# Retiming the later batches of a fused retention and Fourier-mixing kernel, with more of the ReLU on ScalarE

## The chip, the cores and the metric

One core of one Trainium2 chip. The metric is the device time of one execution in microseconds (us). A kernel's time is the median of its executions. Engines are named as the profile names them: PE (TensorE), PEld (its weight loads), DVE (VectorE), ACT (ScalarE), POOL (GpSimd) and SP, whose queue (SPq) issues almost all transfers. A "psh product" is a matmul of the first layer, a "psc product" one of the second; "wkA" is the score product q k^T.

## The reference, cut to what matters

```python
# retention: q, k, v are (4 batches, 8 heads, 768 steps, 64), float32
for t in range(S):
    state = gamma * state + outer(k[:, :, t], v[:, :, t])
    y[:, :, t] = scale * q[:, :, t] @ state
x = y.transpose(0, 2, 1, 3).reshape(B, S, 512)
# Fourier mixing, normalisation and a two-layer MLP with residual
u  = x + real(fft(fft(x, axis=1), axis=2))
un = (u - mean(u)) / sqrt(var(u) + 1e-6)
out = u + relu(un @ w_ch1) @ w_ch2        # w_ch1 512x2048, w_ch2 2048x512
```

The kernel computes the recurrence in chunks: scores of 128 x 128 under a decay mask, and a running state. The Fourier transform is a set of products with cosine and sine tables. Tiles are float16, sums float32. The attention of batch b+1 is woven into the MLP of batch b. That is why nearly all products are ready in time, and why the order of instructions decides where PE waits.

## The kernel before

Units of work are put into one order by time slots: every stream of units gets a start and an end in "batches", and the units are sorted by slot. Each engine then works through its own instructions in that order, as far as the scheduler of the build leaves it. The parts that the change touches:

```python
    def load_unit(b, i, after=None):
        def run():
            h0 = 2 * PAIR_ORDER[i]
            for name, src in srcs.items():
                t = inp.tile([P, 2, NCH, D], f32, tag="in32", name=f"{name}32")
                rows = "h (p c) d -> p h c d" if b < NPE and name == "q" else \
                    "h (c p) d -> p h c d"
                dma = nc.sync.dma_start(t, src[b, h0:h0 + 2].rearrange(rows, p=P))
                if after is not None:
                    tc.add_manual_dep(dma.ins, w_dma[after].ins.name,
                                      mybir.DependencyInfo(mybir.DependencyClass.Sync,
                                                           mybir.DependencyReason.DATA),
                                      reason="loads in turn")
                in_of[name, b, i] = t
        return run
    # ... cut ...
    def t_unit(b, i):
        def run():
            st = at[b, i] = {}
            kT = st["kT"] = tp.tile([P, NCH, P], f16, tag="kT", name="kT")
            if b >= NPE:
                qT = st["qT"] = qts[i % 2]
                nc.sync.dma_start_transpose(qT.rearrange("p h c t -> p (h c) t"),
                                            q16_of[b, i].rearrange("p h c d -> p (h c d)"))
                nc.sync.dma_start_transpose(kT, kd_of[b, i].rearrange("p c h d -> p (c h d)"))
                return
    # ... cut ...
    def a_unit(b, i, part):
        def run():
            st = at[b, i]
            if part == 0:
                st["atm"] = ap_.tile([P, NCH, 2, P], f16, tag="atm", name="atm")
            wk = ps_g.tile([P, 2, 2, P], f32, tag="g", name="wkA")
            for c2 in range(2):
                c = 2 * part + c2
                nc.tensor.matmul(wk[:, c2], st["kT"][:, c, :], st["qT"][:, :, c, :],
                                 start=True, stop=True)
            nc.vector.tensor_tensor(
                out=st["atm"][:, 2 * part:2 * part + 2], in0=wk,
                in1=maskp[:, PAIR_ORDER[i]].unsqueeze(1).to_broadcast([P, 2, 2, P]),
                op=ALU.mult)
        return run
    # ... cut ...
            if b == 0 and kb < 3:
                for c0, c1 in (((0, 256), (256, DM)) if kb == 0 else ((0, DM),)):
                    una = nc.scalar.activation(un[:, c0:c1], u[:, kb, c0:c1], AF.Identity,
                                               bias=fd[0]["mu"][:, kb:kb + 1], scale=-1.0)
                lb[b]["bst", kb] = bst
    # ... cut ...
    def unT_unit(b, kb):
        def run():
            un, unT = lb[b].pop(("un", kb)), lb[b]["unT"]
            if b >= NPE:
                nc.sync.dma_start_transpose(unT[:, :, kb * P:(kb + 1) * P], un)
                return
            pst = ps_g.tile([P, 4, P], f16, tag="g", name="pst", padded_shape=[P, 8, P])
            for cb in range(4):
                nc.tensor.transpose(pst[:, cb, :], un[:, cb * P:(cb + 1) * P], ident16)
            if b == 0 and kb == 0:
                nc.scalar.copy(unT[:, 0:2, 0:P], pst[:, 0:2])
                nc.scalar.copy(unT[:, 2:4, 0:P], pst[:, 2:4])
            elif (kb % 2 == 0) != (b == 0 and kb < 3):
                nc.vector.tensor_copy(unT[:, :, kb * P:(kb + 1) * P], pst)
            else:
                nc.scalar.copy(unT[:, :, kb * P:(kb + 1) * P], pst)
        return run
    # ... cut ...
    def h_unit(b, rt, fb):
        def run():
            unT = lb[b]["unT"]
            psh = ps_pm.tile([P, 384], f32, tag="pm", name="psh", padded_shape=[P, DM])
            for cb in range(4):
                nc.tensor.matmul(psh, w116[:, cb, fb * P:(fb + 1) * P],
                                 unT[:, cb, rt * 384:(rt + 1) * 384],
                                 start=(cb == 0), stop=(cb == 3))
            if fb % 2 == 0:
                nc.scalar.activation(ht16[:, fb, :], psh, AF.Relu, bias=0.0, scale=-1.0)
            else:
                nc.vector.tensor_scalar(out=ht16[:, fb, :], in0=psh, scalar1=-1.0, scalar2=0.0,
                                        op0=ALU.mult, op1=ALU.max)
        return run
    # ... cut ...
    def ch_unit(b, rt, rb3, part):
        def run():
            rb = rt * 3 + rb3
            if part == 0:
                psc_of[0] = ps_pm.tile([P, DM], f32, tag="pm", name="psc")
            psc = psc_of[0]
            for fb in range(4 * part, 4 * part + 4):
                nc.tensor.matmul(psc, ht16[:, fb, rb3 * P:(rb3 + 1) * P], w216[:, fb, :],
                                 start=(fb == 0), stop=(fb == NFB - 1))
            if part == 3:
                ob = obp.tile([P, DM], f32, tag="ob", name="ob")
                nc.vector.scalar_tensor_tensor(out=ob, in0=psc, scalar=lb[b]["st"][:, rb, 3:4],
                                               in1=lb[b]["u"][:, rb, :], op0=ALU.mult,
                                               op1=ALU.add)
                nc.sync.dma_start(out[b, rb * P:(rb + 1) * P, :], ob)
        return run
    # ... cut ...
    def emit(streams):
        ev = []
        for si, (units, t0, t1) in enumerate(streams):
            for i, u in enumerate(units):
                ev.append((t0 + (t1 - t0) * (i + 1.0) / len(units), si, i, u))
        ev.sort(key=lambda e: e[:3])
        for e in ev:
            e[3]()
            if e[0] < 1.0:
                behind()
                pin(None if e[0] < 0.05 else ["Pool", "GpSimd"])
    # ... cut ...
        t0 = b + (0.1 if b == 0 else 0.0)
        s2s, unTs = mix_units(b, [3, 4, 5])
        streams += [(majors, b, b + 1.0), (s2s, t0 + 0.02, t0 + 0.14),
                    (unTs, t0 + 0.2, t0 + 0.28)]
        if b + 1 < B:
            steps = attn_steps(b + 1)
            if b == 0:
                streams.append(([load_unit(1, i, 6) for i in range(4)], -0.1, 0.0))
                streams.append(([qt_zeros], 0.1, 0.15))
                streams.append(([pad_unit], 0.9, 0.95))
                ts = (0.28, 0.33, 0.38, 0.46, 0.55, 0.63, 0.69, 0.75)
            else:
                streams.append(([load_unit(b + 1, i) for i in range(4)], b - 0.3, b + 0.15))
                n = [len(u) for u in steps]
                ts = [0.04 + 0.55 * sum(n[:j]) / sum(n) for j in range(7)]
                ts.insert(1, ts[1])
            streams.append((steps[0], b + ts[0], b + ts[1]))
            streams += [(u, b + ts[j + 2], b + ts[j + 3]) for j, u in enumerate(steps[1:])]
            end = b + ts[-1]
            streams.append(([s1_unit(b + 1, 0, 1), s1_unit(b + 1, 1, 1)], end + 0.02, end + 0.04))
            s2s, unTs = mix_units(b + 1, [0, 1, 2])
            t1, t2 = (0.13, 0.19) if b == 0 else (0.17, 0.23)
            streams += [(s2s, end + 0.06, end + t1), (unTs, end + t1 + 0.01, end + t2)]
    emit(streams)
```

`load_unit` loads q, k and v of a pair of heads; in batch 2 (b = 1) the loads wait only for the seventh weight load. `t_unit` transposes q (after ACT's cast to float16) and k, for batches 3 and 4 by DMA on SP's queue. `h_unit` is one block of the first layer, whose ReLU goes in turn to ACT and DVE. `ch_unit` is one row block of the second layer, with one eviction of 512 columns and one write at its end. `csn_unit` (not shown) makes one of three small cosine tables on ACT. A `filler` is one product without use that keeps PE working.

## Time and profile before

| | kernel before |
|---|---|
| median of 4 runs beside the changed kernel | 262.43 us (261.95 to 264.47) |
| span in the profiled run | 260.5 us, clock 1.00 |
| first product of the first layer starts at | 34.99 us |
| last product of the second layer ends, roughly | 256.6 us |
| waits for transposed q at wkA | 1.61 + 0.93 + 0.46 = 3.0 us idle |

To read it: PE is nearly always busy, so only the places where it waits can be won. The prediction lists them by stage. The idle time in brackets in a timeline is the time before an instruction in which its engine did nothing, and behind the arrow stands what ended it. One reading is used all through this document, and the prediction derives it: **a stage's loss** is the sum of start-to-start distances of its matmuls, less the time in which those matmuls stream without a pause (216 ns for 512 columns).

### The profile page before, as it was taken

Reading aid. Unit: us, or ns where it says so; the run is one execution under the profiler, and the core shown is the slowest. Engines: PE = TensorE matmul, PEld = TensorE weight load, DVE = VectorE, ACT = ScalarE, POOL = GpSimd, SP = SyncE. Lnnn points to the kernel's source line nnn. Section 1 sums busy time; section 2 is a strip of 40 time slices with the busy share of each in tenths; the row PEclk is TensorE's granted clock in tenths of the full one; section 3 lists DMA queues with packets and bytes.
Section 4 is the critical chain, followed back from the end, with each engine's and each line's share of the span. In section 5 each row is a group of like instructions: output and inputs, shape, how many; then the busy total and the mean of one; then the engine's idle time right before and its main releaser. Section 6 shows DMA issues by size and latency. Waiting matters only on the chain.

```text
span 260.5 us, 5236 instructions
## 1 busy us (share of the span) xinstructions
PE 241.7 (93%) x2020; PEld 145.7 (56%) x2020; DVE 182.5 (70%) x446; ACT 117.9 (45%) x244; POOL 73.1 (28%) x129
## 2 busy tenths in 40 slices
PE   6997899999998989799999998899999999999993
PEld 2454679656766536465566545655566455545541
DVE  7789867978998765897787726897787537423421
ACT  7898576653652345653144406551145315403300
POOL 6758302575100071570001604540003203100000
PEclk9999999999999999999999999999999999999999
DMA  8998999999999209999990185685110431311012
GB/s 172 264 248 136 204 202 207 234 245 261 267 216 224 60 0 248 165 201 185 260 238 3 40 191 117 117 113 131 43 40 0 60 121 25 43 72 49 0 43 81
DMA packets 97432, 35.99 MB, mean 138 GB/s; under 512 B 88192, under 2 KB 94336, under 8 KB 97408
## 3 DMA queue, kind: packets, MB, share of 16 engines
q1 hardware_dynamic: 93184, 31.47, 58.1%
q0 software_dynamic: 4224, 4.19, 9.9%
q8 instruction: 16, 0.26, 0.4%
q14 instruction: 8, 0.07, 0.1%
HBM read 27.26 MB, written 6.29 MB: 129 GB/s over the span
## 4 chain that ended last, share of the span: by engine, by line
PE 54%; DVE 18%; ACT 7%; POOL 7%; DMA 6%; SPq 3%; issue 3%; POOLq 0%; ACTq 0%
PE psc L896 23%; PE psh L859 16%; DMA qTz<-q16z 4%; SPq L153 3%; ACT x L627 3%; PE ps L685 3%; POOL u L795 3%; DVE atm L568 3%; DVE bst L812 2%; DMA k<-in_k_dram 2%; POOL u L793 2%; DVE xab L644 2%; PE wkA L566 2%; DVE ht L865 2%; DVE eo L654 2%
## 5 line engine op out<-in xcount | busy, mean ns | idle before, releaser
L896 PE MATMUL psc<-w,ht 128*128 128x512 f16 x384 | 89.7, 379 | 0.0
L859 PE MATMUL psh<-unT,w 128*128 128x384 f16 x448 | 82.7, 326 | 1.8 <-ACT ht L863 1.1
L859 PEld LDWEIGHTS <-w 128*128 128x128 f16 x448 | 42.6, 98 | 25.7 <-issue 2.8
L896 PEld LDWEIGHTS <-ht 128*128 128x128 f16 x384 | 36.5, 98 | 36.6
L863 ACT ACTIVATE ht<-psh 128x384 f16<-128x384 f32 x56 | 27.4, 488 | 53.9 <-PE psh L859 53.9
L793 POOL TENSOR_TENSOR u<-u,x 128x256 f32<-128x256 f32 x21 | 13.3, 635 | 125.7 <-DVE u L786 122.1
L865 DVE TENSOR_SCALAR ht<-psh 128x384 f16<-128x384 f32 x56 | 30.8, 551 | 11.7 <-PE psh L859 11.4
L900 DVE SCALAR_TENSOR_TENSOR ob<-psc,stats,u 128x512 f32<-128x512 f32 x24 | 17.9, 747 | 25.8 <-PE psc L896 25.8
L568 DVE TENSOR_TENSOR atm<-wkA,maskp 128x512 f16<-128x512 f32 x36 | 23.6, 681 | 2.1 <-PE wkA L566 2.1
L627 ACT ACTIVATE x<-wkY,gexp 128x384 f16<-128x384 f32 x24 | 12.8, 580 | 22.8 <-PE wkY L619 22.8
L814 ACT ACTIVATE un<-u,stats 128x512 f16<-128x512 f32 x21 | 15.1, 720 | 15.8 <-DVE stats L813 13.0
L812 DVE BATCH_NORM_STATS2 bst<-u 128x6 f32<-128x512 f32 x21 | 14.6, 695 | 9.4 <-POOL u L795 9.3
L594 DVE SCALAR_TENSOR_TENSOR s<-s,gkrow,wkK 128x128 f16<-128x128 f16 x48 | 16.3, 339 | 1.0
L566 PE MATMUL wkA<-qTz,kT 128*128 128x256 f16 x72 | 12.6, 272 | 3.2 <-DMA qTz<-q16z 3.0
L139 PE MATMUL wps<-ht 128*128 128x512 f16 x40 | 13.5, 444 | 2.2 <-POOL ht L184 2.2
L349 POOL TENSOR_SCALAR kd<-k,gexp 128x384 f16<-128x384 f32 x24 | 13.7, 583 | 1.8 <-DMA k<-in_k_dram 1.8
L795 POOL TENSOR_TENSOR u<-u,x 128x256 f32<-128x256 f32 x21 | 13.3, 635 | 2.5 <-DVE u L788 2.5
L786 DVE SCALAR_TENSOR_TENSOR u<-pq,g,qn 128x257 f32<-128x257 f32 x24 | 11.4, 475 | 3.4 <-ACT qn L783 3.4
L783 ACT COPY qn<-pq 128x255 f32<-128x255 f32 x24 | 8.8, 369 | 6.5 <-PE pq L774 5.7
L566 PEld LDWEIGHTS <-kT 128*128 128x128 f16 x72 | 6.8, 97 | 8.7 <-issue 4.7
L876 PE MATMUL psh<-unT,w 128*128 128x128 f16 x192 | 11.5, 219 | 0.1
L690 ACT CAST g<-ps 128x386 f16<-128x386 f32 x8 | 4.8, 600 | 14.9 <-PE ps L685 14.9
(144 smaller groups left out, 321.3 us busy)
## 6 DMA issues: line engine op xcount, KB each, us to landing
q<-in_q_dram SPq DMA_DIRECT2D x16, 384.0 KB, 6.1
k<-in_k_dram SPq DMA_DIRECT2D x16, 384.0 KB, 5.6
v<-in_v_dram SPq DMA_DIRECT2D x16, 384.0 KB, 6.3
out_dram<-ob SPq DMA_DIRECT2D x24, 256.0 KB, 2.3
w<-in_moe_w_ch_dram POOLq DMA_DIRECT2D x8, 512.0 KB, 10.9
unT<-un SPq DMA_TRANSPOSE x12, 2.5
kT<-kd SPq DMA_TRANSPOSE x8, 3.0
qTz<-q16z SPq DMA_TRANSPOSE x8, 4.1
```

The lines of the kernel that those rows point to most:

```text
L566: nc.tensor.matmul(wk[:, c2], st["kT"][:, c, :], st["qT"][:, :, c, :], start=True, stop=True)
L568: nc.vector.tensor_tensor(out=st["atm"][:, 2 * part:2 * part + 2], in0=wk, in1=maskp[:, PAIR_ORDER[i]].unsqueeze(1).to_broadcast([P, 2, 2, ...
L594: nc.vector.scalar_tensor_tensor(out=s16[:, c], in0=s16[:, c - 1], scalar=gkrow[:, hp, 1:2], in1=wk[:, c - c0], op0=ALU.mult, op1=ALU.add)
L627: nc.scalar.activation(dst, yk[h2], AF.Copy, bias=0.0, scale=gq8[:, h:h + 1])
L793: nc.gpsimd.tensor_tensor(out=u[:, kb, 0:256], in0=u[:, kb, 0:256], in1=x[:, kb, 0, 1:257], op=ALU.add)
L795: nc.gpsimd.tensor_tensor(out=u[:, kb, 256:512], in0=u[:, kb, 256:512], in1=x[:, kb, 1, 257:1:-1], op=ALU.add)
L812: nc.vector.bn_stats(bst, u[:, kb, :])
L859: nc.tensor.matmul(psh, w116[:, cb, fb * P:(fb + 1) * P], unT[:, cb, rt * 384:(rt + 1) * 384], start=(cb == 0), stop=(cb == 3))
L863: nc.scalar.activation(ht16[:, fb, :], psh, AF.Relu, bias=0.0, scale=-1.0)
L865: nc.vector.tensor_scalar(out=ht16[:, fb, :], in0=psh, scalar1=-1.0, scalar2=0.0, op0=ALU.mult, op1=ALU.max)
L896: nc.tensor.matmul(psc, ht16[:, fb, rb3 * P:(rb3 + 1) * P], w216[:, fb, :], start=(fb == 0), stop=(fb == NFB - 1))
L900: nc.vector.scalar_tensor_tensor(out=ob, in0=psc, scalar=lb[b]["st"][:, rb, 3:4], in1=lb[b]["u"][:, rb, :], op0=ALU.mult, op1=ALU.add)
```

## The change

The intent is to remove PE's waits in batches 2 to 4 without changing the arithmetic: (1) slots are shifted, above all so that the casts and DMA transposes of q come earlier (`ts`, loads, `da`, `dm`); (2) ACT takes 11 and 10 of each 16 ReLU blocks in place of 8, to relieve DVE; (3) the loads of batch 2 also wait for a product of the first batch, so that they do not compete with the weights; (4) the very last row block is done in two column halves, so that half of its eviction and write is out of the way early. At the start (5) the cosine tables move back to the end of the fourth pair, fillers are added, and the first centred row is no longer halved.

```diff
+ACT_ROWS = ((2, 3, 4, 5, 6, 7, 8, 9, 10, 13, 14), (0, 1, 4, 6, 7, 9, 10, 11, 12, 14))
@@ loads
-                    tc.add_manual_dep(dma.ins, w_dma[after].ins.name,
-                                      mybir.DependencyInfo(mybir.DependencyClass.Sync,
-                                                           mybir.DependencyReason.DATA),
-                                      reason="loads in turn")
+                    for x in (w_dma[after].ins, lb[0]["mm"].ins):
+                        tc.add_manual_dep(dma.ins, x.name,
+                                          mybir.DependencyInfo(mybir.DependencyClass.Sync,
+                                                               mybir.DependencyReason.DATA),
+                                          reason="loads in turn")
@@ first centred row of batch 1
-                for c0, c1 in (((0, 256), (256, DM)) if kb == 0 else ((0, DM),)):
-                    una = nc.scalar.activation(un[:, c0:c1], u[:, kb, c0:c1], AF.Identity,
-                                               bias=fd[0]["mu"][:, kb:kb + 1], scale=-1.0)
+                una = nc.scalar.activation(un, u[:, kb, :], AF.Identity,
+                                           bias=fd[0]["mu"][:, kb:kb + 1], scale=-1.0)
@@ its transposed copy
-            if b == 0 and kb == 0:
-                nc.scalar.copy(unT[:, 0:2, 0:P], pst[:, 0:2])
-                nc.scalar.copy(unT[:, 2:4, 0:P], pst[:, 2:4])
-            elif (kb % 2 == 0) != (b == 0 and kb < 3):
+            if (kb % 2 == 0) != (b == 0 and kb < 3):
@@ ReLU
-            if fb % 2 == 0:
+            if fb in ACT_ROWS[rt]:
@@ first layer of batch 1: remembers a product that the loads wait for
+            if (kb, g) == (1, 3):
+                lb[0]["mm"] = mm
@@ second layer: last row block in column halves
+            split = b == B - 1 and rb == NCH - 1
+            n = 2 if split else 4
+            if part % n == 0:
                 psc_of[0] = ps_pm.tile([P, DM], f32, tag="pm", name="psc")
             psc = psc_of[0]
-            for fb in range(4 * part, 4 * part + 4):
-                nc.tensor.matmul(psc, ht16[:, fb, rb3 * P:(rb3 + 1) * P], w216[:, fb, :],
-                                 start=(fb == 0), stop=(fb == NFB - 1))
-            if part == 3:
+            c0, c1 = (256 * (part // 2), 256 * (part // 2) + 256) if split else (0, DM)
+            k0 = NFB // n * (part % n)
+            for fb in range(k0, k0 + NFB // n):
+                nc.tensor.matmul(psc[:, c0:c1], ht16[:, fb, rb3 * P:(rb3 + 1) * P],
+                                 w216[:, fb, c0:c1], start=(fb == 0), stop=(fb == NFB - 1))
+            if part % n == n - 1:
                 ob = obp.tile([P, DM], f32, tag="ob", name="ob")
-                nc.vector.scalar_tensor_tensor(out=ob, in0=psc, scalar=lb[b]["st"][:, rb, 3:4],
-                                               in1=lb[b]["u"][:, rb, :], op0=ALU.mult,
+                nc.vector.scalar_tensor_tensor(out=ob[:, c0:c1], in0=psc[:, c0:c1],
+                                               scalar=lb[b]["st"][:, rb, 3:4],
+                                               in1=lb[b]["u"][:, rb, c0:c1], op0=ALU.mult,
                                                op1=ALU.add)
-                nc.sync.dma_start(out[b, rb * P:(rb + 1) * P, :], ob)
+                nc.sync.dma_start(out[b, rb * P:(rb + 1) * P, c0:c1], ob[:, c0:c1])
@@ start: the three csn units go from pairs 2 and 3 to the end of pair 4 (other moves cut)
-        un += a(1) + [csn_unit(0), filler(1), kv0_unit(1)] + e(1, *std) + [sc_unit(1)]
-        un += [q0_unit(2), t0_unit(2, 0), te_unit(2, 0), csn_unit(1), filler(3), k0_unit(2),
-               t0_unit(2, 1), te_unit(2, 1)]
+        un += a(1) + [filler(1), kv0_unit(1)] + e(1, *std) + [sc_unit(1)]
+        un += [q0_unit(2), t0_unit(2, 0), te_unit(2, 0), filler(3), k0_unit(2), t0_unit(2, 1),
+               te_unit(2, 1)]
# ... cut ...
+        un += a(3) + e(3, (0, 0), (1, 0)) + [kv0_unit(3), filler(4), sc_unit(3), t_act(4, 2),
+                                             csn_unit(0), csn_unit(1), csn_unit(2)]
# ... cut: four more fillers, folds in another order ...
@@ time slots of the streams
-        t0 = b + (0.1 if b == 0 else 0.0)
         s2s, unTs = mix_units(b, [3, 4, 5])
-        streams += [(majors, b, b + 1.0), (s2s, t0 + 0.02, t0 + 0.14),
-                    (unTs, t0 + 0.2, t0 + 0.28)]
+        dm = (0.12, 0.24, 0.3, 0.38) if b == 0 else (0.004, 0.140, 0.200, 0.341)
+        streams += [(majors, b, b + 1.0), (s2s, b + dm[0], b + dm[1]),
+                    (unTs, b + dm[2], b + dm[3])]
         if b + 1 < B:
             steps = attn_steps(b + 1)
             if b == 0:
-                streams.append(([load_unit(1, i, 6) for i in range(4)], -0.1, 0.0))
+                streams.append(([load_unit(1, i, 6) for i in range(4)], 0.180, 0.220))
                 streams.append(([qt_zeros], 0.1, 0.15))
-                streams.append(([pad_unit], 0.9, 0.95))
-                ts = (0.28, 0.33, 0.38, 0.46, 0.55, 0.63, 0.69, 0.75)
+                streams.append(([pad_unit], 0.900, 0.950))
+                ts = (0.249, 0.368, 0.424, 0.429, 0.545, 0.630, 0.695, 0.750)
             else:
-                streams.append(([load_unit(b + 1, i) for i in range(4)], b - 0.3, b + 0.15))
-                n = [len(u) for u in steps]
-                ts = [0.04 + 0.55 * sum(n[:j]) / sum(n) for j in range(7)]
-                ts.insert(1, ts[1])
+                streams.append(([load_unit(b + 1, i) for i in range(4)], b + -0.249, b + 0.044))
+                n = [len(u) for u in steps[1:]]
+                ts = [0.040, 0.044] + [0.044 + 0.550 * sum(n[:j]) / sum(n)
+                                         for j in range(6)]
             streams.append((steps[0], b + ts[0], b + ts[1]))
             streams += [(u, b + ts[j + 2], b + ts[j + 3]) for j, u in enumerate(steps[1:])]
             end = b + ts[-1]
-            streams.append(([s1_unit(b + 1, 0, 1), s1_unit(b + 1, 1, 1)], end + 0.02, end + 0.04))
+            da = (0.040, 0.048, 0.105, 0.135, 0.187, 0.237) if b == 0 else \
+                (0.068, 0.072, 0.054, 0.164, 0.174, 0.196)
+            streams.append(([s1_unit(b + 1, 0, 1), s1_unit(b + 1, 1, 1)], end + da[0],
+                            end + da[1]))
             s2s, unTs = mix_units(b + 1, [0, 1, 2])
-            t1, t2 = (0.13, 0.19) if b == 0 else (0.17, 0.23)
-            streams += [(s2s, end + 0.06, end + t1), (unTs, end + t1 + 0.01, end + t2)]
+            streams += [(s2s, end + da[2], end + da[3]), (unTs, end + da[4], end + da[5])]
```

More of the change, by code (lines that the diff above doesn't have):

```diff
@@ L875, in run @@
                 for cb in range(4):
-                    nc.tensor.matmul(psh[:, f], w116[:, cb, fb * P:(fb + 1) * P],
-                                     unT[:, cb, kb * P:(kb + 1) * P],
-                                     start=(cb == 0), stop=(cb == 3))
+                    mm = nc.tensor.matmul(psh[:, f], w116[:, cb, fb * P:(fb + 1) * P],
+                                          unT[:, cb, kb * P:(kb + 1) * P],
+                                          start=(cb == 0), stop=(cb == 3))
+            if (kb, g) == (1, 3):
+                lb[0]["mm"] = mm
             dst = ht16[:, 4 * g:4 * g + 4, kb * P:(kb + 1) * P]
@@ L891, in run @@
             rb = rt * 3 + rb3
-            if part == 0:
+            split = b == B - 1 and rb == NCH - 1
+            n = 2 if split else 4
+            if part % n == 0:
                 psc_of[0] = ps_pm.tile([P, DM], f32, tag="pm", name="psc")
             psc = psc_of[0]
-            for fb in range(4 * part, 4 * part + 4):
-                nc.tensor.matmul(psc, ht16[:, fb, rb3 * P:(rb3 + 1) * P], w216[:, fb, :],
-                                 start=(fb == 0), stop=(fb == NFB - 1))
-            if part == 3:
+            c0, c1 = (256 * (part // 2), 256 * (part // 2) + 256) if split else (0, DM)
[4 more added lines that the diff above has]
+            if part % n == n - 1:
                 ob = obp.tile([P, DM], f32, tag="ob", name="ob")
-                nc.vector.scalar_tensor_tensor(out=ob, in0=psc, scalar=lb[b]["st"][:, rb, 3:4],
-                                               in1=lb[b]["u"][:, rb, :], op0=ALU.mult,
+                nc.vector.scalar_tensor_tensor(out=ob[:, c0:c1], in0=psc[:, c0:c1],
+                                               scalar=lb[b]["st"][:, rb, 3:4],
+                                               in1=lb[b]["u"][:, rb, c0:c1], op0=ALU.mult,
                                                op1=ALU.add)
-                nc.sync.dma_start(out[b, rb * P:(rb + 1) * P, :], ob)
+                nc.sync.dma_start(out[b, rb * P:(rb + 1) * P, c0:c1], ob[:, c0:c1])
         return run
@@ L975, in first_units @@
                                                                      half_ids]
-        un += a(1) + [csn_unit(0), filler(1), kv0_unit(1)] + e(1, *std) + [sc_unit(1)]
-        un += [q0_unit(2), t0_unit(2, 0), te_unit(2, 0), csn_unit(1), filler(3), k0_unit(2),
-               t0_unit(2, 1), te_unit(2, 1)]
+        un += a(1) + [filler(1), kv0_unit(1)] + e(1, *std) + [sc_unit(1)]
+        un += [q0_unit(2), t0_unit(2, 0), te_unit(2, 0), filler(3), k0_unit(2), t0_unit(2, 1),
+               te_unit(2, 1)]
         un += y(1) + [td_dve(0), td_dve(1), yx_unit(1), filler(2)] + x(1) + [
             gk_unit(o[2]), t_act(3, 0), t_act(3, 1), v0_unit(2)]
-        un += a(2) + [filler(1), kv0_unit(2)] + e(2, *std) + [sc_unit(2), t_act(3, 2),
-                                                              csn_unit(2)]
+        un += a(2) + [filler(1), kv0_unit(2)] + e(2, *std) + [sc_unit(2), t_act(3, 2)]
         un += [q0_unit(3), w1_unit(0), t0_unit(3, 0), te_unit(3, 0), filler(3)] + y(2)
@@ L987, in first_units @@
         un += [w1_unit(g) for g in range(1, 4)] + [w2_unit(g) for g in range(4)]
-        un += a(3) + e(3, (0, 0), (1, 0)) + [kv0_unit(3), filler(4), sc_unit(3), t_act(4, 2)]
+        un += a(3) + e(3, (0, 0), (1, 0)) + [kv0_unit(3), filler(4), sc_unit(3), t_act(4, 2),
+                                             csn_unit(0), csn_unit(1), csn_unit(2)]
         un += e(3, (0, 1), (1, 1))
-        un += [yx_unit(3), yi_unit(3, 0), x0_unit(3, 0), filler(1), yi_unit(3, 1), x0_unit(3, 1),
+        un += [yx_unit(3), yi_unit(3, 0), x0_unit(3, 0), filler(2), yi_unit(3, 1), x0_unit(3, 1),
                g0_unit(0, (1,)), filler(1)]
-        un += [fold_s(0, 0, 130, 1, 2), fold_d(0, 0), s1_unit(0, 0, 0), fold_s(0, 130, 258, 1, 2),
-               px_unit(0), fold_d(0, 1, (0,)), xmean_unit(0), fold_d(0, 1, (1,)),
-               s1_unit(0, 1, 0), s1_unit(0, 0, 1), s1_unit(0, 1, 1), g0_unit(0, (2,)),
-               mean_unit(0)]
-        un += [s2_unit(0, 0), px_unit(1), s2_unit(0, 1), norm_unit(0, 0), gr_unit(0), gr_unit(1),
-               px_unit(2), filler(2), unT_unit(0, 0), xmean_unit(1), mean_unit(1),
+        un += [fold_s(0, 0, 130, 1, 2), fold_d(0, 0, (0,)), s1_unit(0, 0, 0),
+               fold_s(0, 130, 258, 1, 2), fold_d(0, 0, (1,)), fold_d(0, 1, (0,)), px_unit(0),
+               xmean_unit(0), fold_d(0, 1, (1,)), s1_unit(0, 1, 0), s1_unit(0, 0, 1),
+               s1_unit(0, 1, 1), px_unit(1), filler(1), g0_unit(0, (2,)), mean_unit(0)]
+        un += [s2_unit(0, 0), s2_unit(0, 1), norm_unit(0, 0), gr_unit(0), gr_unit(1),
+               px_unit(2), filler(4), unT_unit(0, 0), xmean_unit(1), mean_unit(1),
                norm_unit(0, 1), s2_unit(0, 2), xmean_unit(2), mean_unit(2), norm_unit(0, 2),
```

## The prediction

> **What bounds the kernel now.** I read the busy shares first, then the chain that ended last, then the busy times by stage, then TensorE's waits and its timeline around them.
>
> ```profile
> PE 241.7 (93%) x2020; PEld 145.7 (56%) x2020; DVE 182.5 (70%) x446; ACT 117.9 (45%) x244; POOL 73.1 (28%) x129
> ...
> PE 54%; DVE 18%; ACT 7%; POOL 7%; DMA 6%; SPq 3%; issue 3%; POOLq 0%; ACTq 0%
> ```
>
> TensorE is busy for 93% of the span and is the largest part of the last chain, but 46% of the chain lies elsewhere: the chain leaves TensorE wherever TensorE waits. A schedule change can win only those waits. The matmuls hardly change, so I must find the waits and see which of them the new order removes.
>
> ```profile
> 34.99:48.35 13.36, 13.11 (x212) 12.28 (x212) 9.24 (x23) 10.00 (x28) 2.72 (x8) 1.00 1.19 218
> 48.35:63.90 15.55, 14.46 (x121) 8.39 (x119) 12.69 (x31) 7.14 (x11) 10.36 (x15) 1.00 1.18 241
> 63.90:83.00 19.10, 18.22 (x206) 13.16 (x203) 17.74 (x46) 10.21 (x19) 1.98 (x3) 1.00 1.14 241
> 83.00:98.73 15.73, 14.43 (x94) 7.17 (x91) 11.49 (x27) 5.61 (x11) 5.61 (x9) 1.00 0.27 59
> 98.73:116.00 17.27, 15.33 (x129) 10.18 (x128) 13.71 (x34) 10.95 (x24) 9.42 (x15) 1.00 1.08 213
> ...
> 156.00:176.00 20.00, 18.53 (x159) 11.64 (x157) 16.37 (x41) 11.80 (x27) 9.42 (x15) 1.00 0.66 113
> 176.00:200.00 24.00, 23.14 (x193) 14.31 (x193) 18.49 (x43) 7.29 (x15) 1.23 (x2) 1.00 0.22 58
> ```
>
> Columns: stretch, its length, busy us of PE, PEld, DVE, ACT, POOL, clock, DMA share, GB/s. The clock is 1.00 throughout, so none of the loss is throttling. DVE is at 93% in 63.9-83 (17.74 of 19.10) and at 82% in 156-176, ACT at 53% and 59% there.
>
> Busy time hides part of each wait: a 512-column matmul is recorded as 379 ns, but 48 in a row take 10.36 us, 216 ns each, so about 0.16 us of drain covers the start of each pause. I therefore take each matmul's start-to-start distance in the timeline and subtract its streaming time (216 ns for 512 columns, 162 for 384, in proportion otherwise). What is left over per stage: 10.1 us before 35, then 0.9, 1.4, 1.7, 2.3, 2.65 (to 116), 1.1 (to 143), 0, 3.05 (156-176), 1.0, 1.0, and 0 from 225 on. From 35 to 256.6 that is 15.1 us; after the last matmul come 3.9 us of eviction and output.
>
> ```profile
> 107.60 0.38 PE L566 MATMUL wkA<-qTz,kT 128*128 128x256 f16 x2 [1.61 <-DMA qTz<-q16z]
> ...
> 163.11 0.38 PE L566 MATMUL wkA<-qTz,kT 128*128 128x256 f16 x2 [0.93 <-DMA qTz<-q16z]
> ...
> 176.61 0.38 PE L566 MATMUL wkA<-qTz,kT 128*128 128x256 f16 x2 [0.46 <-DMA qTz<-q16z]
> ```
>
> These three waits for a transposed q are the largest late ones: by start-to-start 1.77, 1.09 and 0.63 us, 3.5 in all. The chain shows the first:
>
> ```profile
> 101.28 0.92 PE psh L859 x6
> 102.20 5.26 DMA qTz<-q16z
> 107.47 0.14 issue
> ```
>
> The transpose needs 5.26 us from issue and is issued at 102.20 because ACT's cast of q16z ends only then, behind two ReLUs.
>
> **What the Trainium skill says.** (1) "TensorE: Matmul & The Clock Gate", Part 2, step 1: matmuls stay in program order, only weight loads are pulled ahead. So one waiting score product holds all ready first-layer products behind it; the trace agrees (1.61 us idle, then psh goes on). (2) The same page, Back-to-back issue gap, gives N/2.4 + 2.5 ns warm, 216 at N=512; the trace has 216. Halving 16 matmuls to 32 thus costs an estimated 16 x 2.5 = 40 ns. (3) "VectorE: DVE Perf Modes", The TRN2 errata, has (120+N)/0.96 ns for a PSUM source on VectorE and (172+N)/1.2 on ScalarE, 525 and 463 ns at 384 columns; the trace has 551 and 488, 5% more. (4) "Perfetto Trace Analysis", DMA Instruction HWDGE: the issuing record excludes data movement. The trace agrees: a q transpose is 1.5 us on the queue and 4.1 us to landing, so the landing counts.
>
> ```profile
> L863 ACT ACTIVATE ht<-psh 128x384 f16<-128x384 f32 x56 | 27.4, 488 | 53.9 <-PE psh L859 53.9
> ...
> L865 DVE TENSOR_SCALAR ht<-psh 128x384 f16<-128x384 f32 x56 | 30.8, 551 | 11.7 <-PE psh L859 11.4
> L900 DVE SCALAR_TENSOR_TENSOR ob<-psc,stats,u 128x512 f32<-128x512 f32 x24 | 17.9, 747 | 25.8 <-PE psc L896 25.8
> ```
>
> **The change part by part.** Positions below come from the built instruction order of both kernels, counted in matmul streaming time.
>
> q transposes ahead, batches 3 and 4. For batch 3 the first q cast moves on ACT ahead of the square root and the two ReLUs, so it ends some 3 us earlier, near 99, and the transpose lands near 104; the score product still comes 6.9 us of streaming after the stage's first product (7.0 before), near 105.7. The 1.77 us go. With the untangled groups (wkY no longer splits a psh group, after which 0.42 us waited for ACT) I book **2.0 of 2.65**. For batch 4 the cast and the transpose move into the previous batch; the third pair's product now comes 6.55 us after the buffer's last reader (5.5 before) against the 5.38 us which its DMA took plus hand-over. I book **2.3 of 3.05**.
>
> Second batch. Its first casts hold TensorE at 51.2-53 for 0.64 + 0.79 = 1.42 us; the transposes of q now come 4.8 us of streaming after the second layer starts, 2.8 before. **1.3**. The new load wait: loads started at 42.9, as soon as the seventh weight load landed, competing with the eighth until 44.5; the product named ends near 45. Of the 2 us delay about 1 is real for the stream, and the later casts have 3 to 5 us of slack before their transposes. **0**.
>
> ReLU mostly on ACT: 11 + 10 of 32 in place of 8 + 8. Over batches 2 to 4 that is 5 each and 2 in batch 1: 17 x 0.551 = 9.4 us off DVE, 17 x 0.488 = 8.3 us on ACT. Almost none of it is on the path by itself; it matters where DVE is full. In 63.9-83 one wait for a buffer costs 0.74 us and two for DVE 0.4 and 0.3: **0.9** of 1.7. In 116-143 and 176-200, four waits of 0.31 for atm or the folds: **0.6 + 0.6**. In 200-225: **0.4**. In 83-98.7 three waits for centred rows cost 1.58 us; their distance from the preceding products grows only by 0.3-0.6: **0.5**.
>
> Sum 2.0 + 2.3 + 1.3 + 0.9 + 1.2 + 0.4 + 0.5 = 8.6 us. Some waits will come back a few instructions later, since the chains behind them (u, POOL, bn_stats, ACT) are serial. I keep 85%: **7.3**.
>
> Column halves: the last eviction has 256 columns, 747 - 256/0.96 = 480 ns (estimate), 0.27 less; the last write has 128 KB, an estimated 0.25 less. Less 0.04: **0.5**.
>
> Costs. The three cosine-table activations (0.60 each, about 1.5 back to back) move from places where ACT had slack to right before the fourth pair's x, where ACT was idle 0.65 us: about **0.8** on the path to the first layer. Four more fillers are 4 x 0.216 = 0.86 us, mostly in idle time: **0.3**. ACT: in the first 15 us of batch 2's first half it now has 11 ReLUs (5.0 us at 0.45 back to back), 8 casts (3.7), 3 rows (2.0), 3 qn (1.1), x and unT (1.6): 13.4 of about 15.5 us, in order, with centred rows waiting on DVE among the ReLUs: **0.9** of new waits. Costs 2.0.
>
> Net 7.3 + 0.5 - 2.0 = 5.8 us: 262.4 - 5.8 = **256.6 us**.
>
> **Rivals.** *ACT takes DVE's place.* Runs of up to nine ReLUs in a row stand on ACT between centred rows that wait for statistics; if a row is late, three psh buffers are soon full and TensorE stops. For it: 13.4 of 15.5 us. Against: DVE, on which the rows wait, loses 1.65 us in the same stretch. It would give back 3 us or so: about 260. *Later transposes only move the wait.* The transposes share DMA with loads (213 GB/s in 98.7-116); if the earlier transpose takes 7 us rather than 5.3, half of the 3.5 us stays: about 258.5. *The full gain.* All stage losses but the 10 us at the start shrink to small change and cosines cost nothing: 15.1 less some 5, plus the tail: about 252.5.
>
> **Range and chances.** The first two rivals together would give about 261, the third 252.5; 8 in 10 I put at 253.3 to 260.3. Faster by 2% is below 257.1, just above my value: 0.54. Slower by 2% needs more new waits than all of ACT's added work: 0.02. The rest 0.44.
>
> **What would show it.** Right: no wait of wkA for qTz over 0.5 us; stage from first psh to the second layer of batch 2 near 15.3 us streaming plus 0.7; DVE near 173 us, ACT near 126; no wait over 0.3 us at tq of batch 2; first layer starts 0.5-1 us later than 34.99; last matmul to end 3.4 us. Wrong: psh waiting for ht on ACT by over 2 us in total (the first rival); transposes landing after 6 us and wkA still waiting (the second); first layer starting at 35 or before, with late losses under 6 us (the third).

## The result, and the profile after

The changed kernel takes **254.17 us** (median of 4 runs, 254.16 to 254.27) against 262.43 us beside it. It is correct. The ratio is 0.967, with a 95% interval of 0.962 to 0.972; a second measurement in five rounds gave 0.970 (0.969 to 0.971). Ratios here are the mean time of one kernel's fast runs over that of the other's fast runs of the same rounds, so not quite the ratio of the medians that are quoted. The gain is 8 us; 5.8 were predicted.

Busy shares, then the chain that ended last by engine, of the kernel after:

```profile
PE 237.9 (94%) x2040; PEld 147.7 (59%) x2040; DVE 176.1 (70%) x430; ACT 124.9 (49%) x259; POOL 73.1 (29%) x129
...
PE 68%; DVE 11%; ACT 7%; DMA 6%; POOL 3%; SPq 2%; issue 2%; ACTq 0%; DVEq 0%
```

PE's part of the last chain rose from 54% to 68% and DVE's fell from 18% to 11%: the chain leaves PE less often. PE's busy time fell by 3.8 us although it ran 20 more matmuls (16 by halving, 4 fillers). No work was saved there: a matmul ahead of a pause is recorded with its drain, and there are fewer pauses. This is a reason to read start-to-start distances.

Busy times by stage after, with the columns that the prediction explains. The first four stages answer to the first four rows of before, the fifth to 98.73-116.00, the sixth to the first-layer part of 156-176:

```profile
35.91:49.12 13.21, 12.96 (x213) 12.29 (x213) 9.37 (x23) 9.72 (x27) 2.72 (x8) 1.00 0.96 179
49.12:64.36 15.24, 15.23 (x138) 9.29 (x136) 13.37 (x35) 8.19 (x14) 9.78 (x15) 1.00 1.19 243
64.36:81.52 17.16, 16.87 (x187) 12.24 (x185) 15.78 (x40) 10.09 (x19) 2.62 (x4) 1.00 1.25 243
81.52:96.89 15.37, 14.55 (x96) 7.52 (x95) 11.31 (x27) 6.50 (x13) 5.61 (x9) 1.00 0.51 110
96.89:112.76 15.87, 15.02 (x134) 10.23 (x132) 13.53 (x34) 11.52 (x27) 9.37 (x15) 1.00 1.24 214
151.53:166.06 14.53, 14.53 (x127) 10.10 (x126) 12.90 (x32) 10.93 (x26) 9.44 (x15) 1.00 0.46 97
```

The third row took 19.10 us before and takes 17.16. Two of these stages (49.12 and 151.53) have no idle PE left at all. Worked out by stage from the two traces (loss as defined above, us; "booked" is the prediction's figure before its discount):

| stage | before | after | change | booked |
|---|---|---|---|---|
| first layer of batch 1 | 0.88 | 0.73 | -0.15 | - |
| second layer, batch 1, first half | 1.44 | 0.34 | -1.10 | 1.3 |
| batch 1, second half, first layer | 1.69 | 0.65 | -1.04 | 0.9 |
| its second layer | 2.27 | 1.58 | -0.69 | 0.5 |
| batch 2, first half, first layer (attention of batch 3) | 2.65 | 1.15 | -1.50 | 2.0 |
| its second layer and the next first layer | 1.11 | 0.39 | -0.72 | 0.6 |
| batch 3, first half, both layers (attention of batch 4) | 3.35 | 1.18 | -2.17 | 2.3 |
| batch 3, second half, first layer | 0.70 | 0.21 | -0.49 | 0.6 |
| batch 4, first half, first layer | 0.99 | 0.49 | -0.50 | 0.4 |
| **sum** | **15.1** | **6.7** | **-8.4** | **8.6** |

The prediction booked by slightly different stretches, so its figures answer to these rows only roughly. The first layer starts 0.92 us later, at 35.91. At the end about half a microsecond is won. 8.4 - 0.9 + 0.5 = 8.0, the difference of the spans (260.5 and 252.5).

PE's timeline at wkA after, which answers to the three waits shown before:

```profile
104.95 0.61 PE L568 MATMUL wkA<-qTz,kT 128*128 128x256 f16 x4 [0.85 <-DMA kT<-kd]
...
169.39 0.38 PE L568 MATMUL wkA<-qTz,kT 128*128 128x256 f16 x2 [0.81 <-DMA qTz<-q16z]
```

Two of three waits are left, 1.66 us idle in place of 3.0, and the first is now for k and not for q. In the chain of waits the k transpose stands where the q transpose stood:

```profile
98.97 0.70 SPq L516
...
99.72 5.19 DMA kT<-kd
...
104.95 0.61 PE wkA L568 x4
```

The groups of the ReLU and the last evictions after (line, operation, tile, count; busy us, mean ns; idle before and its end):

```profile
L861 ACT ACTIVATE ht<-psh 128x384 f16<-128x384 f32 x73 | 34.4, 489 | 32.2 <-PE psh L857 31.3
...
L904 DVE SCALAR_TENSOR_TENSOR ob<-psc,stats,u 128x512 f32<-128x512 f32 (+1 forms) x25 | 18.2, 726 | 26.4 <-PE psc L900 26.4
L863 DVE TENSOR_SCALAR ht<-psh 128x384 f16<-128x384 f32 x39 | 21.4, 552 | 10.1 <-PE psh L857 9.7
```

17 ReLU blocks moved to ACT (73 in place of 56, 39 in place of 56 on DVE); each costs what it did before. The last evictions stand in DVE's timeline, before and after:

```profile
256.55 0.75 DVE L900 SCALAR_TENSOR_TENSOR ob<-psc,stats,u 128x512 f32<-128x512 f32 x1 [2.70 <-PE psc L896]
```

```profile
247.38 0.48 DVE L904 SCALAR_TENSOR_TENSOR ob<-psc,stats,u 128x256 f32<-128x256 f32 x1 [1.00 <-PE psc L900]
249.12 0.48 DVE L904 SCALAR_TENSOR_TENSOR ob<-psc,stats,u 128x256 f32<-128x256 f32 x1 [1.26 <-PE psc L900]
```

From the end of the last eviction to the end of the span it was 3.2 us (257.30 to 260.5) and is 2.9 (249.60 to 252.5).

### The profile page after: what moved, and what is told of

Its sections match the earlier page's. It is cut to its first block, busy times and chain, and to the rows that moved or that the text cites. A ratio compares the mean times of both kernels' runs of the same rounds, so it can differ in the third digit from the quotient of the medians.

```text
span 252.5 us, 5283 instructions
## 1 busy us (share of the span) xinstructions
PE 237.9 (94%) x2040; PEld 147.7 (59%) x2040; DVE 176.1 (70%) x430; ACT 124.9 (49%) x259; POOL 73.1 (29%) x129
## 4 chain that ended last, share of the span: by engine, by line
PE 68%; DVE 11%; ACT 7%; DMA 6%; POOL 3%; SPq 2%; issue 2%; ACTq 0%; DVEq 0%
PE psc L900 29%; PE psh L857 21%; PE psh L874 3%; PE ps L687 3%; DMA k<-in_k_dram 2%; PE wkA L568 2%; DMA kT<-kd 2%; DMA qTz<-q16z 2%; SPq L154 2%; DVE atm L570 1%; PE pq L776 1%; PE wkY L621 1%; PE pq L772 1%; ACT un L815 1%; PE wkY L617 1%
## 5 line engine op out<-in xcount | busy, mean ns | idle before, releaser
L900 PE MATMUL psc<-w,ht 128*128 128x512 f16 (+1 forms) x400 | 89.3, 370 | 0.0
L900 PEld LDWEIGHTS <-ht 128*128 128x128 f16 x400 | 38.1, 98 | 35.5
L857 PEld LDWEIGHTS <-w 128*128 128x128 f16 x448 | 42.9, 98 | 24.1 <-issue 0.7
L861 ACT ACTIVATE ht<-psh 128x384 f16<-128x384 f32 x73 | 34.4, 489 | 32.2 <-PE psh L857 31.3
L795 POOL TENSOR_TENSOR u<-u,x 128x256 f32<-128x256 f32 x21 | 13.4, 637 | 116.1 <-DVE u L788 111.3
L904 DVE SCALAR_TENSOR_TENSOR ob<-psc,stats,u 128x512 f32<-128x512 f32 (+1 forms) x25 | 18.2, 726 | 26.4 <-PE psc L900 26.4
L863 DVE TENSOR_SCALAR ht<-psh 128x384 f16<-128x384 f32 x39 | 21.4, 552 | 10.1 <-PE psh L857 9.7
L815 ACT ACTIVATE un<-u,stats 128x512 f16<-128x512 f32 x21 | 15.1, 721 | 14.5 <-DVE stats L814 8.6
L874 PEld LDWEIGHTS <-w 128*128 128x128 f16 x192 | 11.0, 98 | 0.8 <-issue 0.7
L790 DVE SCALAR_TENSOR_TENSOR u<-pq,g,qn 128x255 f32<-128x255 f32 x24 | 11.3, 469 | 0.0
## 6 DMA issues: line engine op xcount, KB each, us to landing
out_dram<-ob SPq DMA_DIRECT2D x23, 256.0 KB, 2.2
```

The costliest lines, as they stand in the source:

```text
L815: una = nc.scalar.activation(un, u[:, kb, :], AF.Identity, bias=stats[:, kb, 0:1], scale=-1.0)
L857: nc.tensor.matmul(psh, w116[:, cb, fb * P:(fb + 1) * P], unT[:, cb, rt * 384:(rt + 1) * 384], start=(cb == 0), stop=(cb == 3))
L874: mm = nc.tensor.matmul(psh[:, f], w116[:, cb, fb * P:(fb + 1) * P], unT[:, cb, kb * P:(kb + 1) * P], start=(cb == 0), stop=(cb == 3))
L900: nc.tensor.matmul(psc[:, c0:c1], ht16[:, fb, rb3 * P:(rb3 + 1) * P], w216[:, fb, c0:c1], start=(fb == 0), stop=(fb == NFB - 1))
L904: nc.vector.scalar_tensor_tensor(out=ob[:, c0:c1], in0=psc[:, c0:c1], scalar=lb[b]["st"][:, rb, 3:4], in1=lb[b]["u"][:, rb, c0:c1], op0=AL ...
```

## The experiments

My theory when they began: the prediction's parts are all real, and the gain is larger than predicted because the discount of 15% and the 0.9 us of new ACT waits did not come. The rivals: one part earned nearly everything and the others nothing; or some parts (the load wait, the cosine tables) cost time that others hide.

Each edit below is relative to the changed kernel unless noted. To compare runs I use the ratios: 0.970 for the changed kernel (the five-round measurement), and 0.001 of ratio is 0.26 us. Not undone alone were the new slot of batch 2's loads, the four fillers and the reordered folds.

### Repeated measurement of the changed kernel

No edit.

> The changed kernel itself, for a closer ratio and as the mark for the other three runs of this call. Ratio to the kernel before 0.966 to 0.970.

Measured 254.37 us, ratio 0.970 (0.969 to 0.971). This is the value that the others are held against.

### ReLU undone, and ReLU alone

```diff
-            if fb in ACT_ROWS[rt]:
+            if fb % 2 == 0:
```

> The changed kernel with the ReLU split as before (even rows on ACT, odd on DVE). My theory (parts add up; ReLU off DVE was booked at 2.5 us of regained waits, 2.1 after the 15% discount): 256.3 us, 255.8 to 256.8, with waits of 0.3 us for atm and for the folds back in the batches' second halves and one of 0.5 to 0.7 for a psh buffer near 78 us. Rival A (only the new order of transposes and casts matters): 254.2 within 0.4. Rival B (the ReLU is the root and the new order works only with DVE relieved): 258 or more, waits for qTz back.

Measured 255.93 us, ratio 0.9765 (0.975 to 0.978): undoing it costs 1.7 us, as expected. By stage the loss returns in the second half of batch 1 (0.65 to 1.29), in the first layer of batch 4 (0.49 to 1.11) and by 0.18 twice in between, but not in the stages that run the attention of batches 3 and 4 (2.41 against 2.33 together).

ReLU alone is the same line changed in the kernel before, with `ACT_ROWS`, and nothing else:

> The kernel before with the new ReLU split and nothing else. My theory: 262.4 less about 2 = 260.4 us (259.9 to 261.0); the three waits of wkA for qTz (1.6, 0.9, 0.5 us idle) stay. Rival A (order only): 262.4 within 0.5. Rival B (ReLU is the root): 257 or less, waits for qTz shorter by half.

Measured 259.06 us, ratio 0.988 (0.986 to 0.989): 3.2 us gained, more than the 1.7 that are lost when it is undone last. Here the same three attention stages lose 4.2 in place of 6.0 us. So their waits had two cures: less work on DVE, or better slots. **The parts overlap**, and their gains must not be added. What the ReLU does not cure is the wait for q; the timeline of PE with the ReLU alone:

```profile
106.94 0.38 PE L567 MATMUL wkA<-qTz,kT 128*128 128x256 f16 x2 [1.64 <-DMA qTz<-q16z]
...
161.61 0.38 PE L567 MATMUL wkA<-qTz,kT 128*128 128x256 f16 x2 [0.95 <-DMA qTz<-q16z]
```

These are the waits of the kernel before, unchanged.

ReLU undone also gives a clean measure of what moving it does to the engines, since all else is equal:

```profile
PE 240.2 (94%) x2040; PEld 148.2 (58%) x2040; DVE 181.7 (71%) x447; ACT 117.5 (46%) x242; POOL 73.2 (29%) x129
```

ACT gains 124.9 - 117.5 = 7.4 us for 17 blocks, but DVE loses only 181.7 - 176.1 = 5.6 us, 0.33 us a block and not the 0.55 of its record. Busy time is a union, and records overlap: in the timeline a ReLU on DVE recorded with 0.55 us is often followed after 0.46. Summed record by record, the ReLUs on DVE do lose 9.3 us; 3.1 of them had overlapped other records.

### Slots of batches 3 and 4 undone

```diff
-                streams.append(([load_unit(b + 1, i) for i in range(4)], b + -0.249, b + 0.044))
-                n = [len(u) for u in steps[1:]]
-                ts = [0.040, 0.044] + [0.044 + 0.550 * sum(n[:j]) / sum(n) ...
+                (loads b - 0.3 to b + 0.15, ts, da and dm of b > 0 as in the kernel before)
```

> The changed kernel with all emission times of batches 3 and 4 as before (attention steps, their loads, first and second half of the mixing), the rest of the change kept. My theory: 254.2 + 3.5 to 4.5 = 257.7 to 258.7 us, with wkA waiting for qTz by 2.5 to 3 us in total. Rival B (DVE relief shortens these waits by itself): 255 to 256, waits for qTz under 1.5 us in total.

Measured 257.8 us, ratio 0.984 (0.981 to 0.987): 3.7 us lost, the largest single part, as expected. PE's timeline has the waits for q back:

```profile
106.22 0.38 PE L568 MATMUL wkA<-qTz,kT 128*128 128x256 f16 x2 [2.10 <-DMA qTz<-q16z]
...
160.84 0.38 PE L568 MATMUL wkA<-qTz,kT 128*128 128x256 f16 x2 [0.92 <-DMA qTz<-q16z]
```

To see which of the slots does it, two halves of it alone. First the steps (`ts` for b > 0) as before, the loads, `da` and `dm` as after:

> The changed kernel with the emission times of the attention steps of batches 3 and 4 as before; their loads and mixing keep the new times. My theory (the earlier q casts and transposes carry most of the 4.4 us which all late times are worth): 2.5 to 4 us slower than the changed kernel, waits of wkA for qTz over 1.5 us in total. Rival (the loads being out of the transposes' way carries it): under 1 us slower.

Measured 258.0 us (257.34 to 259.57), ratio 0.9845: all of the loss, within the interval. But it is not the same loss: of the expected waits of wkA for q none is left. The profile is of the slowest of the four runs (259.57, the others took 257.3 to 258.0), so it shows more loss than a typical run has. PE's timeline:

```profile
103.12 0.44 PE L586 MATMUL wkK<-v,kd 128*128 128x128 f16 x5 [1.17 <-POOL v L356]
...
109.13 0.39 PE L568 MATMUL wkA<-qTz,kT 128*128 128x256 f16 x2 [1.19 <-DMA kT<-kd]
```

Both come once more in batch 4's attention (1.17 and 0.81 us). Waiting for v's cast on POOL is new; neither full kernel has such a wait among those over half a microsecond. POOL works in order too: with old steps and new mixing slots its casts of the first pair start at 101.12 behind additions that wait for DVE, against 93.91 in the changed kernel. So the slots are one tuned set, and undoing one of them measures a mixture that nobody had tuned. The step is needed; its own worth cannot be read from this run.

Second the loads alone (`b - 0.3, b + 0.15` again):

> The changed kernel with the emission times of the loads of batches 3 and 4 as before; steps and mixing keep the new times. My theory: 0 to 1 us slower. Rival (loads in the way of the transposes are what cost): 2 us slower or more, with landings of the transposes longer than 5 us.

Measured 254.49 us, ratio 0.970 (0.969 to 0.971): nothing. When the loads of batches 3 and 4 are issued does not matter for the time within this range. Inside, a wait changed places: the k transpose of batch 3 goes out earlier (95.17) and no product waits for it, but wkA waits 1.11 us for q's transpose, and the stage loses 1.28 us, as much as in the changed kernel (1.15 and 1.27 in its two profiles).

### Slots of batch 2 undone

The steps and the mixing rows only; its loads keep their new slot.

```diff
-                ts = (0.249, 0.368, 0.424, 0.429, 0.545, 0.630, 0.695, 0.750)
+                ts = (0.28, 0.33, 0.38, 0.46, 0.55, 0.63, 0.69, 0.75)
-            da = (0.040, 0.048, 0.105, 0.135, 0.187, 0.237) if b == 0 else \
+            da = (0.02, 0.04, 0.06, 0.13, 0.14, 0.19) if b == 0 else \
```

> The changed kernel with the emission times of the second batch's attention and mixing as before. My theory: the wait of tq for POOL's casts comes back, now longer since the loads start 1 to 2 us later: 254.2 + 1.3 to 2.3 = 255.5 to 256.5 us. Rival (that wait was hidden behind DVE work in the same stretch): 254.2 within 0.5.

Measured 256.0 us, ratio 0.976 (0.975 to 0.978): 1.6 us, as expected. The loss returns where it was: 0.34 to 1.33 in the second layer of batch 1, 0.65 to 1.15 and 1.58 to 2.05 in the two stages after. PE waits again at its transposes of batch 2, 0.6 us for k's cast and 0.4 for q's.

### Cosine tables back

```diff
-        un += a(1) + [filler(1), kv0_unit(1)] + e(1, *std) + [sc_unit(1)]
+        un += a(1) + [csn_unit(0), filler(1), kv0_unit(1)] + e(1, *std) + [sc_unit(1)]
         (csn_unit(1) and csn_unit(2) to their old places in the same way)
```

> The changed kernel with the three cosine-table activations back at their old places. My theory (they sit on the path before the fourth pair's x and cost 0.8 us): 0.5 to 0.9 us faster than the changed kernel, 253.3 to 253.7, first product of the first layer near 35.1 in place of 35.9 us. Rival (the later start comes from the fillers and from the undivided centred row): within 0.2 us of the changed kernel.

Measured 253.94 us, ratio 0.968 (0.967 to 0.970): 0.4 us gained, half of what was expected. The move costs time, and the timelines show where. First the changed kernel on PE, then this one:

```profile
27.83 0.33 PE L722 MATMUL ps<-xg,csn 128*128 128x4 f16 x7 [0.32 <-ACT csn L270]
...
29.89 0.69 PE L687 MATMUL ps<-ssp,eo 128*128 128x193 f16 x6 [0.54 <-DVE eo L656]
...
35.91 2.84 PE L874 MATMUL psh<-unT,w 128*128 128x128 f16 x48 [0.23 <-ACT unT L848]
```

```profile
27.39 0.37 PE L722 MATMUL ps<-xg,csn 128*128 128x4 f16 x9
...
29.36 0.69 PE L687 MATMUL ps<-ssp,eo 128*128 128x193 f16 x6
...
35.36 2.84 PE L874 MATMUL psh<-unT,w 128*128 128x128 f16 x48 [0.23 <-ACT unT L848]
```

In the changed kernel ACT makes the three tables from 26.16 to 27.77 and the fourth pair's x after that. PE waits for the tables and then for DVE's folds of x, and the first layer starts 0.55 us later than with the tables in their old places.

### Load wait undone

```diff
-                    for x in (w_dma[after].ins, lb[0]["mm"].ins):
+                    for x in (w_dma[after].ins,):
```

> The changed kernel with the second batch's loads waiting for the seventh weight load only. My theory: nothing, within 0.3 us of the changed kernel, since the casts have 3 to 5 us of slack. Rival 1 (the wait keeps the loads from slowing the eighth weight load, which the second layer needs): 0.5 us slower or more, with a wait of psc for w. Rival 2 (the wait only delays the casts): 0.5 us faster.

Measured 253.68 us, ratio 0.967 (0.966 to 0.969): 0.7 us gained. My theory (nothing) fell. The rival's number fits, but not its place: it saw the cost at the casts of batch 2, and up to there the stage losses of the two traces agree. The loss falls in the first layer of batch 2, where the attention of batch 3 runs: 1.15 (1.27 in the second profile of the changed kernel) to 0.59. SP's queue shows what differs, in the changed kernel (start, us, what is issued):

```profile
94.42 0.39 SPq L154 DMA_DIRECT2D k<-in_k_dram  x1
95.08 0.60 SPq L154 DMA_DIRECT2D v<-in_v_dram  x1
97.61 0.36 SPq L908 DMA_DIRECT2D out_dram<-ob  x1
98.08 1.59 SPq L516 DMA_TRANSPOSE qTz<-q16z  x1
99.72 1.63 SPq L518 DMA_TRANSPOSE kT<-kd  x1
```

and without the load wait, with PE's product that needs them in the second fence:

```profile
95.19 0.39 SPq L154 DMA_DIRECT2D v<-in_v_dram  x1
96.85 1.54 SPq L516 DMA_TRANSPOSE qTz<-q16z  x1
98.53 0.74 SPq L908 DMA_DIRECT2D out_dram<-ob  x1
99.32 1.26 SPq L518 DMA_TRANSPOSE kT<-kd  x1
```

```profile
102.39 0.39 PE L568 MATMUL wkA<-qTz,kT 128*128 128x256 f16 x2 [0.41 <-DMA kT<-kd]
```

The k transpose lands 5.19 us after its issue in the changed kernel, and 3.02 us after it without the wait; q's takes 5.47 and 3.76. Two things stand ahead of q's transpose that do not without the wait: one load more of 384 KB, and the output write at 97.61, which waits for its eviction on DVE. ACT's cast of q ends at about the same time in both (96.72 and 96.83 us). Without the wait SP issues the transpose at once (96.85) and the write after it; in the changed kernel the transpose stands behind the write until 98.08. So its later issue (1.2 us) comes from the order on SP's queue and not from late data. The Trainium skill ("DMA: Bandwidth & Descriptors", Queues, rings and completion order) says that each DMA engine consumes the descriptors of a ring in order; the traces fit it: in both, the transfers of this stretch land in the order of their issue (in the changed kernel at 98.44, 100.15, 100.78, 103.55 and 104.91 us). What makes the landings longer is not isolated. It need not be the one load more: in the run with the slots of batch 2 undone a single load is issued in the five us before q's transpose, as without the wait, and k's still takes 5.08 us to land. The wait delays the first load of batch 2 from 42.65 to 45.45 us, and with it the loads after: in the changed kernel SP issues four loads of batch 3 between 86.6 us and the q transpose, without the wait one. What stays open: taking the wait out also changed the order of instructions on SP, ACT, PE and DVE, since the scheduler reorders around it. The 0.7 us are wait and order together.

### Column halves undone

```diff
-            split = b == B - 1 and rb == NCH - 1
+            split = False
```

> The changed kernel with the last rows in one eviction and one write of 512 columns. My theory: 0.4 to 0.6 us slower; end of the last matmul to the end of the span 4.0 in place of 3.4 us. Rival (the write has a fixed latency, so only the eviction shrinks): 0.25 us slower.

Measured 254.99 us, ratio 0.972 (0.971 to 0.974): 0.6 us, as expected. The last eviction is one of 0.75 us again.

### Both costs taken out, and the first centred row in halves again

Load wait and cosine tables undone together:

> The changed kernel with the load wait of the second batch and the move of the cosine tables both undone. They act in different places (the transposes near 104 us, the start before 35 us), so the gains of 0.7 and 0.4 us should add up: 1.0 to 1.3 us faster than the changed kernel, ratio to the kernel before 0.965 to 0.966, 253.1 to 253.3 us. Rival (the earlier start is given back at the transposes, which do not move): 0.7, as with the load wait alone.

Measured 253.53 us, ratio 0.966 (0.965 to 0.967): 1.0 us better than the changed kernel, nearly the sum of the two (0.4 + 0.7). One more undone, the first centred row and its transposed copy of batch 1 in column halves as before:

```diff
-                una = nc.scalar.activation(un, u[:, kb, :], AF.Identity, ...)
+                for c0, c1 in (((0, 256), (256, DM)) if kb == 0 else ((0, DM),)):
+                    una = nc.scalar.activation(un[:, c0:c1], u[:, kb, c0:c1], AF.Identity, ...)
```

> As the run before, and the first centred row and its transpose's copy in two halves as in the kernel before. Theory that this row in one piece explains the rest of the later start (0.3 us): 0.2 to 0.4 us faster than the run before. Rival (that rest comes from the four more fillers): no difference, within 0.15.

Measured **252.82 us** (252.48 to 253.12), ratio 0.964 (0.9625 to 0.9651). This is the best version: 3.6% faster than the kernel before, and about 1.5 us faster than the changed kernel. The first layer now starts at 34.77 us, 0.75 before that of the run before (35.52; 0.59 before the run with the tables back alone), and a little before the 34.99 of the kernel before. In halves the row's centring starts at 33.06 us, before the second half of u is ready (33.41); from the row's mean to the first product it takes 2.79 us in place of 3.31, so 0.5 of the 0.75 is the row. I had expected 0.2 to 0.4 us; in time it is about 0.6. (The order on SP's queue also differs by one place of one load, which I do not separate. The nine runs of this document whose start is that of the changed kernel begin the first layer anywhere from 35.91 to 36.26 us, so a start is known to a few tenths at best.)

## Why the prediction was right or wrong

The time, 254.2, lies inside the range of 253.3 to 260.3, and faster by over 2% had the largest chance. The mechanism was right, but the size was 2.2 us short (8.0 in place of 5.8), and several terms reached the right sum by the wrong way.

**The discount of 15% and the new ACT waits were the terms that failed in size.** The prediction summed 8.6 us of stage losses, kept 7.3 of them and took off 0.9 more for ACT. The stage losses fell by 8.4: nothing of the sum was given back. And psh waited for a ReLU on ACT for 0.3 us in all after, against 1.1 before: with more ReLU on it, ACT held PE up less. The estimate of 13.4 of 15.5 us counted eight casts of q in that stage (3.7 us); five fall in it (2.4 us). In the profile ACT is busy for 11.52 of 15.87 us there. The first rival, ACT in DVE's place, is refuted by that. Without those two terms the prediction's own figures give 8.6 + 0.5 - 1.1 = 8.0, which is what was measured.

**q transposes ahead: booked 2.0 + 2.3, measured 1.5 + 2.2 in these stages,** and yet the sign "no wait of wkA for qTz over 0.5 us" failed (0.81 at 169.39), with a new one for kT (0.85). The second rival, that the wait only moves, was half right: by idle time 1.66 of 3.0 us stay. The steps that failed are these. For batch 3 the q transpose landed where it was told (103.55, "near 104"), but the product was held to come near 105.7; the stage itself started 1.85 us earlier (96.88 in place of 98.73), so it was due at 104.1, and the k transpose, which the prediction did not follow, landed last (104.91). For batch 4's third pair the room of 6.55 us was set against 5.38 and an unsized hand-over: q's transpose was issued at 164.36, 2.7 us after the buffer's last reader (161.65) and right behind k's on SP's queue, and took 4.90, 7.6 in all. The rest of what these stages gained, some 2 us (3.7 less the 1.5 or so that wkA gained, start to start), came from other waits there, which the ReLU alone also cures. The prediction counted the ReLU only in other stages. That is why ReLU alone gave 3.2 us and undoing it last costs 1.7.

**Second batch: booked 1.3, measured 1.1 by stage**; undoing its slots costs 1.6 in all, with 0.5 each in the two stages after, where the prediction had put the gain down to the ReLU and to centred rows. No wait at the transposes of q in batch 2 is left over 0.3 us, as the sign said.

**ReLU: the 9.4 us off DVE were mis-sized.** 5.6 came off, since records overlap (DVE is at 176.1 and not "near 173"). On ACT 8.3 were told and 7.4 came (124.9, "near 126").

**Load wait: booked 0, measured 0.7 us of cost.** The step looked for the cost at the casts of batch 2, which indeed have slack. It did not follow the queue further: the delay goes on to the loads of batch 3, and the order on SP's queue around two transposes changes with it. Which of the two costs how much stays open.

**Start: 0.8 + 0.3 booked, 0.92 measured, from other terms.** The cosine tables cost 0.55 us at the first product (0.4 in time), and the first row in one piece costs 0.6, which the prediction did not book although the diff shows it. The two full kernels say the same: the row's mean comes 0.48 us later (32.59 for 32.11) and the way from there to the first product takes 0.44 longer (3.32 for 2.88). As the version with both undone starts 0.22 us before the kernel before, with all four fillers in it, the fillers and the reordered folds together cost nothing that these runs can tell.

**Halves: booked 0.5, measured 0.6.** The eviction of 256 columns was estimated at 480 ns and took 0.48 us; what follows it, estimated at 0.25 less without a working, took 0.3 less (3.2 to 2.9).

**One sign held by luck.** The stage of batch 2 was told "near 15.3 us streaming plus 0.7" and took 15.87, but as 14.7 of streaming and 1.15 of loss.

**The third rival, the full gain at 252.5**, was nearest on the upper side: the losses did shrink to small change, but the start was not free. With the start's costs and the load wait taken out it was nearly reached: 252.8.

## What to carry to other kernels

Where one busy engine works in order, list the losses by stage from start-to-start distances, and test a discount before you take it (here 8.4 of 8.6 us came); but do not add what two cures of the same wait earn. Test each part of a tuned change by undoing it: here three of its parts (a wait on loads, moved tables, a joined row) cost 1.5 us together, and without them the kernel was better than either version. A transfer's cost is not only at its own consumer: look at what stands ahead of it on its queue. Here a transpose whose input was ready at 96.72 us was issued at 98.08, behind an output write.

## What the Trainium skill lacked or had wrong

- "TensorE: Matmul & The Clock Gate", Back-to-back issue gap, gives about 131 ns per matmul at N=512 for a sustained stream of weight loads and matmuls. In both kernels 48 such pairs in a row take 10.36 us, 216 ns each. The formula that the page calls isolated is the one that held.
- "VectorE: DVE Perf Modes", The TRN2 errata: (120+N)/0.96 ns is short by a fixed amount for an operation with two tensors, one in PSUM, and a scalar: 747 against 658 ns at 512 columns, 480 against 392 at 256. For the one-input ReLU at 384 columns it is 552 against 525.
- "DMA: Bandwidth & Descriptors" gives a bandwidth for DMA transposes (261 GB/s in one kernel), but no time from issue to landing of one transpose among other transfers. For the k tile of 768 x 128 float16 (0.75 us at that bandwidth, an estimate) it was 3.02 us in the run without the load wait and 5.19 in the changed kernel.
